# Where the loads of k, q and v and two rows of a weight product stand in a gated attention with a multiplicative FFN

## The chip, the core and the metric

The kernel runs on one core of one Trainium2 chip, in fp32. The metric is the device time in microseconds of one execution; the time before is the median of three runs. One further execution was taken with the hardware profiler, and every view below comes from it. Its engines are TensorE (PE; its weight loads are shown as PEld), VectorE (DVE), ScalarE (ACT), GpSimd (POOL) and SyncE (SP), whose queue issues nearly all DMAs.

## The reference

Attention, over 4 batches, 8 heads, 768 steps and a head size of 48, keeps a complex state S for each head. The bridge lays the heads side by side (384 columns, 3072 tokens), and the FFN multiplies two projections before two more weights.

```python
mag = np.sqrt(a_re * a_re + a_im * a_im)
scale = np.minimum(mag, 0.999) / (mag + 1e-06)
ar, ai = a_re * scale, a_im * scale
for t in range(S):
    kv = k[:, :, t] outer v[:, :, t]
    S_re, S_im = ar[t] * S_re - ai[t] * S_im + kv, ar[t] * S_im + ai[t] * S_re
    y[:, :, t] = q[:, :, t] @ S_re
x = y as (3072, 384)
out = ((x @ w1) * (x @ w2) @ w3) @ w_out      # w1, w2: 384 x 1024; w3: 1024 x 1024; w_out: 1024 x 384
```

The weights arrive as 64-bit floats and are read as pairs of 32-bit words ("words" below).

## The kernel before

**Algebra.** w3 @ w_out is computed once (`fuse`) and kept as `w3o`, so the FFN of a unit is two projections, their product `ab`, and one product with `w3o`. The gates are turned into cumulative magnitudes and angles, and k and q are scaled and rotated by them; attention is then a masked product in chunks of 128 steps with a carried state T.

**Units.** Work is cut into 8 units u = 0 to 7 (a batch and half its steps, 384 tokens, 3 chunks c). For a unit there are:

- the gates' passes (`gates(u)`, on ACT and DVE, 128 x 1152 each, in this order: a1, r1, im, sq, z1, n, z2, a2, z3, min, three mag scans, l, e, at, z4, r2, three ang scans, turns, k, q, ends, z5, abs, cos, sin, kc, qc, ks, qs), and then the moves: 12 DMAs of 192 KB that write KL and QL from R, k, A and q (L724);
- the pieces on PE (`pieces(u)`): tr (`turn`, transposes of R and k, L754, copied to KT by ACT, L756), kv (`state`, L818, and a DVE addition L824), sc (`scores`, L768, two halves for each chunk, each followed by DVE's COPY_PREDICATED into A, L771), and y (`outputs`, L801, copied to xT by ACT, L803). sc20 is chunk 2, half 0; y2 is chunk 2. One sc is 32 MATMULs and 32 LDWEIGHTS, one y 64 and 64 (y0 of an even unit 32 and 32), one kv 48 and 48, one tr 3 and 3;
- the FFN on PE: 16 items ab1, ab2 (`ffn_ab`, L840; 6 MATMULs each; ACT copies the first, DVE multiplies the second into `ab`, L845 and L847; four PSUM buffers m), then the products with w3o: for unit 0 six half items o (8 MATMULs each, L931), from unit 1 on one o and seven p (L895).

**Order.** In the first stage the 8 rows of w3 and w_out are loaded (`row_load`), rounded to fp32 by DVE and ACT (`row_work`, L975 to L992) and multiplied into eight PSUM sums (`fuse(f, j)` is row f, sum j, L1126, two MATMULs and two LDWEIGHTS), between the steps of unit 0's gates. Of rows 6 and 7 only j 0 to 3 are done there; the other halves are "fills" of two j each (f6 and f7) between unit 0's pieces. Two of the sums lie in the PSUM banks of sc, two in those of tr, kv and y, four in m. After row 7 ACT copies each sum to `w3o` (L1130).

The second stage is one list `seq` of PE items: unit 0's pieces with the fills, `begin 0`, unit 0's 16 ab items, then for each unit its pieces mixed with FFN items of the unit before. `FILLS` says ahead of which piece the fills of unit 0 and the six o items in unit 1 stand. In unit u > 1, AHEAD[u] FFN items come ahead of the pieces; unit 1 does not read AHEAD. `run` issues the items in that order, and after item number n as many steps of other work as `PLAN[n]` has letters: c the next pass of the gates, u the next step of rounding w1 and w2 (`w12_ops`; signs, ends, shifted, rounded), o a step of `out_weights`. After PLAN's end a planner with costs and due times chooses. At "need u" all passes of unit u that are left are issued; its moves are only issued once unit u-1 has ended.

w1 and w2 are cut into 4 blocks n, of which w1's and w2's words come as two DMAs (`w12_load`; 768 KB each for whole blocks); ab item 4n is the first to read block n. The words go through two buffers, so block n + 2 is requested when block n is rounded. The first part of block 0 lies in the buffers that unit 1's q and k take afterwards.

SP's queue takes each DMA in program order: an issue that waits for a buffer holds up those behind it. k and q of a unit are three DMAs of 192 KB each (`load_qkv`), v comes once as `vr` (`load_v`, 576 KB) for kv and once turned into Vb (`turn_v`, 14 DMAs of 18 to 72 KB) for y. Two places matter here: k and q of unit 1 were loaded after the second rounding of w12_ops,

```python
                if (parts, k) == (got[0][1][0], 1):
                    load_qkv(1)
```

and those of unit u + 1 right behind the moves of unit u, V of unit u + 1 at "begin u".

Of the kernel before, what the change touches and what calls it, by code (L numbers as in the profile page):

```python
# [375 lines left out]
def kernel(  # L376
# [45 lines left out]
    KF = FF // P  # L422
# [5 lines left out]
    TT = S // 2  # L428
    UC = TT // C
    NU = 2 * B  # L430
    AHEAD = [0, 0, 12, 10] + [8] * (NU - 4)
    LO, HI = 32, D - 32
    PASS, WIDE, SCAN, LAND, SLACK, LATE, RING, LOOK, NEAR, EARLY = 1.17, 1.4, 1.05, 1.8, 0.7, 1.2, 8, 4.0, 4, 2
    LOOKS = 3
    PLAN = ("c uuu uucc - - - cu uu cu cu uuu c u c u cu cu - u uuuuuc u - - uuu c cuu ccuc ucucc ucc uuuuuu "
            "ccccc - - ccc uc ccc c - - - - c - - - c - c c - c c cc - - - ccccccc - - c - ccc ccc cc - c - "
            "ccccccc - cc - - - - - ").split()
    FILLS = [1, 9, 14, 19], [3, 4, 6, 11, 14, 16]
    SB, LANES = 32, C // 32
    LN_EPS = math.log(1e-6)  # L440
    PI = math.pi
# [122 lines left out]
    def gates(u, split):  # L564
# [60 lines left out]
        for s in parts:  # L625
# [2 lines left out]
            yield "ACT", PASS, "e", ("l",)  # L628
            act(out=r[:, s], in_=r[:, s], func=AF.Exp, scale=-1.0)
        yield None  # L630
        q, K2 = g["q"], g["k"]
        k = K2[:, :, 0:TT]

# [99 lines left out]
                tt(out=q[:, s], in0=q[:, s], in1=Z[:, s], op=OP.mult)  # L733
            move(QL, (A, q), s)
        landed("moves", ("ks", "qs"), 4 * KD, 0.95)
        if 1 < u + 1 < NU:
            load_qkv(u + 1)
        yield None

    def step(ops, n=1):  # L740

        for _ in range(n):
            for op in ops:
                if op is None or op == "move":
                    break
# [63 lines left out]
    def state(u, c):  # L809

        KT, V = KT_t.pop((u, c)), g_t[u]["vr"][:, c].rearrange("p (h d) -> p h d", d=D)
        n = u % 2 * UC + c
        T = T_t.get((u // 2, n))
        kv = ps_v.tile([2 * D, H, D], FP, tag="v", name="kv")
        for hd in range(H):
            rows = KT[:, hd].rearrange("p d x f -> p (d x f)")
            for g in range(0, 2 * D, SB):
                nc.tensor.matmul(out=kv[g:g + SB, hd], lhsT=rows[:, g:g + SB], rhs=V[:, hd], start=True, stop=True)  # L818
        Tn = Tb[(u * UC + c) % 3]
        with tc.high_priority():  # L820
            if T is None:
                nc.scalar.copy(out=Tn[:, :, 0:D], in_=kv)
            else:
                nc.vector.tensor_tensor(out=Tn[:, :, 0:D], in0=kv, in1=T[:, :, 0:D], op=OP.add)  # L824
        if c == UC - 1:
            rho = L_t[u][1][:, :, TT:TT + 1].to_broadcast([2 * D, H, D])
            nc.vector.tensor_tensor(out=Tn[:, :, 0:D], in0=Tn[:, :, 0:D], in1=rho, op=OP.mult)
        T_t[u // 2, n + 1] = Tn
        if u + 1 < NU and c == UC - 1 - u % 2:
            load_v(u + 1)  # L830

    def ffn_ab(u, j):
# [257 lines left out]
    def w12_ops():  # L1090
        for n in range(FF // WB):
            for parts, k, raw in got[n]:
                ready["raw"] = ready[("raw", n)]
                yield from weight_ops((w1s, w2s)[k][:, n, parts], raw)
                if (parts, k) == (got[0][1][0], 1):
                    load_qkv(1)
            rounded[0] += 1
            w12_load(n + 2)

    def row_load(f, parts=1):  # L1100

# [147 lines left out]
    def run(seq):  # L1249
# [81 lines left out]
            o[0] = next(o[1])  # L1331
        for k, (kind, f) in enumerate(seq):
            if kind == "begin":
                if f + 1 < NU:
                    turn_v(f + 1)
                    landed("V", (), 14, 0.3, 0.57)
                held["unit"] = f
                others.extend([next(o), o] for u, o in streams if u == f)
            elif kind == "need":
                while gate["u"] <= f and gate["op"]:  # L1340
                    book(gate["op"])
                    advance()
                clock["PE"] = max(clock["PE"], ready.get("ks", 0.0))
                held.update(tr=[], kv=0)
            elif kind == "end":
                ended[0] = f
                if gate["op"] == "move":
                    advance()
            elif kind == "judge":
                for _ in looks[0]:  # L1350
                    pass
                judge(f)
            else:
                if kind == "sc":
                    clock["PE"] = max(clock["PE"], ready["moves"])
                item(kind)
                f()
                if k >= len(PLAN):
                    fill(k)
                while looks and held["unit"] > 1 and clock["POOL"] < clock["PE"] and next(looks[0], "over") != "over":  # L1360
                    clock["POOL"] = max(clock["POOL"], clock["PE"] - LOOK) + LOOK
# [10 lines left out]
    with tc.manual_schedule(engines={mybir.EngineType.PE}):  # L1372
# [9 lines left out]
        for f in range(KF):  # L1382
# [5 lines left out]
            if f == VLOAD:  # L1388
                load_v(0)
                w12_early()  # L1390
            if f >= KF - 2:
                continue
            for j in range(KF):
                fuse(f, j)
            step(steps, (3, 2, 2, 2, 1, 1)[f])
        for _ in steps:
            pass
        for f in range(KF - 2, KF):
            for j in range(KF // 2):
                fuse(f, j)  # L1400
        fills = [("f7" if f == KF - 1 else "f", lambda f=f, j=j: [fuse(f, j + x) for x in range(2)])
                 for f in range(KF - 2, KF) for j in range(KF // 2, KF, 2)]
        gate["ops"] = gates(1, False)
        chain(nc.scalar.preload_act_table_set("natural_log_exp_and_others"))
        with tc.manual_schedule(engines={mybir.EngineType.Activation, mybir.EngineType.DVE, mybir.EngineType.Pool, mybir.EngineType.SP}):
# [69 lines left out]
```

## Time and profile before

| What | Value |
|---|---|
| median of three runs | 557.94 us (557.38 to 559.2) |
| the profiled execution | 558.92 us, span 557.0 us, mean granted clock 0.99 |
| PE busy | 521.9 us, 94% of the span, 5474 MATMULs and 5474 LDWEIGHTS |
| DVE, ACT, POOL busy | 358.0, 272.7, 358.7 us |
| DMA queue q1 (SP), q0 (POOL) | 69.78 MB, 19.01 MB |
| DMA queue q8, instructions | 45 packets, 0.74 MB |
| first ab item of unit 0 (L840) | 88.43 us |
| first ab item of unit 1 | 152.93 us |
| first tr of unit 2 | 178.08 us |

Times inside a profile count from the first instruction, and the time of an execution is 1.9 us more than its span here. In a line of a timeline the start comes first and then the duration; in the chain of waits each line is a start, a duration and what ran or was waited for, and "issue" is time in which the engine waited for nothing that the profile shows. In a table of stages the columns are the stretch, its length, the busy times of PE, PEld, DVE, ACT and POOL with their instruction counts, the granted clock of PE, the DMA share and GB/s. The slices of the page are 13.9 us each.

### The profile page before, as it was taken

How to read it: one execution, taken by the hardware profiler on the slowest of the kernel's cores; microseconds unless marked ns; L12 is line 12 of the kernel's file. 1: busy time of each engine (PE TensorE's matmuls, PEld its weight loads, DVE VectorE, ACT ScalarE, POOL GpSimd, SP SyncE). 2: the span in 40 equal slices, each digit the busy share in tenths (PEclk: the TensorE clock that was granted, in tenths of full speed). 3: DMA queues.
4: the chain of work that ended last, by engine and by line, in shares of the span. 5: the costliest groups of instructions: out<-in, count | busy, mean ns of one | idle time of the engine just before them, and what ended most of it. 6: DMA issues, size and time to landing. Idle time of an engine off the chain costs nothing.

```text
span 557.0 us, 13239 instructions
## 1 busy us (share of the span) xinstructions
PE 521.9 (94%) x5474; PEld 359.1 (64%) x5474; DVE 358.0 (64%) x520; ACT 272.7 (49%) x391; POOL 358.7 (64%) x425
## 2 busy tenths in 40 slices
PE   4688769997999999999999999999999999999995
PEld 2344555565756696558756785679566966696564
DVE  7999576964587778769744984587448851331141
ACT  6988856554644655491628443744367222101100
POOL 1000000088898888889988998889898888887000
PEclk9999998998999999999999999999999999999999
DMA  8999796189359835985498347933793273222001
GB/s 265 358 409 267 159 334 175 44 205 192 102 141 237 203 106 159 223 218 158 113 203 189 98 122 184 235 100 108 155 231 108 82 207 73 72 87 74 0 3 48
DMA packets 73222, 89.73 MB, mean 161 GB/s; under 512 B 31808, under 2 KB 62976, under 8 KB 72384
## 3 DMA queue, kind: packets, MB, share of 16 engines
q1 hardware_dynamic: 67072, 69.78, 47.9%
q0 software_dynamic: 6080, 19.01, 12.0%
q8 instruction: 45, 0.74, 0.6%
q14 instruction: 25, 0.20, 0.1%
HBM read 65.14 MB, written 4.72 MB: 125 GB/s over the span
## 4 chain that ended last, share of the span: by engine, by line
PE 79%; DVE 6%; ACT 6%; DMA 4%; issue 3%; SPq 1%; DVEq 0%; ACTq 0%
PE m L840 40%; PE p L895 12%; PE o L931 10%; PE y L801 7%; PE sc L768 5%; DMA im<-in_a_im_dram 3%; PE kv L818 3%; PE tp L754 2%; ACT gZ L576 2%; ACT low L980 1%; PE f L1126 1%; DMA re<-in_a_re_dram 1%; DVE gZ L675 1%; ACT gA L576 1%; SPq L510 1%
## 5 line engine op out<-in xcount | busy, mean ns | idle before, releaser
L840 PE MATMUL m<-xT,w2s 128*128 128x384 f32 x384 | 135.0, 488 | 0.0
L840 PE MATMUL m<-xT,w1s 128*128 128x384 f32 x384 | 134.6, 487 | 0.0
L840 PEld LDWEIGHTS m<-xT,w1s 128*128 128x128 f32 x384 | 72.5, 190 | 48.1 <-issue 0.5
L840 PEld LDWEIGHTS m<-xT,w2s 128*128 128x128 f32 x384 | 71.5, 190 | 46.2
L1047 POOL TENSOR_SCALAR look<-look 128x256 f32<-128x256 f32 (+1 forms) x84 | 90.4, 1076 | 7.3
L847 DVE TENSOR_TENSOR ab<-m,a 128x384 f32<-128x384 f32 x64 | 35.2, 553 | 87.4 <-PE m L840 79.3
L845 ACT COPY a<-m 128x384 f32<-128x384 f32 x64 | 30.2, 474 | 116.1 <-PE m L840 115.8
L1028 POOL TENSOR_TENSOR seen<-seen,look 128x256 bf16<-128x256 bf16 (+1 forms) x84 | 72.2, 860 | 6.8
L1012 POOL MEMSET seen<- 128x256 bf16 x1 | 0.3, 311 | 106.8 <-DVE w2s L992 106.8
L931 PE MATMUL o<-w3o,ab 128*128 128x384 f32 x160 | 55.8, 499 | 0.0
L1044 POOL TENSOR_TENSOR look<-look 128x256 f32<-128x256 f32 (+1 forms) x72 | 53.8, 747 | 2.1 <-DMA look<-in_w_dram 0.3
L1046 POOL TENSOR_SCALAR look<-look 128x256 f32<-128x256 f32 (+1 forms) x44 | 50.8, 1155 | 3.9 <-DMA look<-in_a_re_dram 0.7
L1023 POOL DMA_DIRECT2D look<-in_w_dram x56 | 33.4, 596 | 16.6 <-POOL seen L1028 16.6
L771 DVE COPY_PREDICATED A<-mask,sc 128x512 f32<-128x512 uint8 x48 | 32.7, 730 | 16.5 <-PE sc L768 16.5
L931 PEld LDWEIGHTS o<-w3o,ab 128*128 128x128 f32 x160 | 30.3, 195 | 19.6 <-issue 1.6
L801 PE MATMUL y<-A,V 128*32 128x128 f32 x768 | 39.3, 274 | 3.1 <-issue 3.1
L1049 POOL TENSOR_TENSOR look<-look 128x256 f32<-128x256 f32 (+1 forms) x44 | 38.8, 883 | 3.7
L768 PE MATMUL sc<-QL,KL 96*32 96x32 f32 (+3 forms) x1536 | 32.6, 236 | 5.7 <-issue 4.2
L803 ACT COPY xT<-y 128x384 f32<-128x384 f32 x24 | 11.4, 474 | 52.8 <-PE y L801 52.7
L801 PEld LDWEIGHTS y<-A,V 128*32 128x32 f32 x768 | 33.8, 110 | 5.0 <-issue 4.4
L1126 PE MATMUL f<-wo_s,w3s 128*128 128x384 f32 x96 | 36.4, 528 | 0.0
L756 ACT COPY KT<-tp 128x384 f32<-128x384 f32 x40 | 34.1, 863 | 4.7 <-PE tp L754 4.7
(123 smaller groups left out, 892.5 us busy)
## 6 DMA issues: line engine op xcount, KB each, us to landing
look<-in_w_dram POOLq DMA_DIRECT2D x56, 256.0 KB, 4.2
raw<-in_w_dram SPq DMA_DIRECT2D x6, 1024.0 KB, 10.2
KL<-gR SPq DMA_DIRECT2D x24, 192.5 KB, 5.5
KL<-k SPq DMA_DIRECT2D x24, 192.5 KB, 6.3
re<-in_a_re_dram SPq DMA_DIRECT2D x24, 192.0 KB, 4.0
im<-in_a_im_dram SPq DMA_DIRECT2D x24, 192.0 KB, 3.6
k<-in_k_dram SPq DMA_DIRECT2D x24, 192.0 KB, 7.8
q<-in_q_dram SPq DMA_DIRECT2D x24, 192.0 KB, 7.5
```

Of the source, the lines that this page charges most:

```text
L768: nc.tensor.matmul(out=sc[SB * g:SB * g + SB, j, s0:C], lhsT=KL[:, x * n + j, w][:, s0:s0 + SB], rhs=QL[:, x * n + j, w][:, s0:C], start=T ...
L801: nc.tensor.matmul(out=o, lhsT=a, rhs=b, start=s0, stop=s1)
L840: nc.tensor.matmul(out=m, lhsT=w[:, j * P // WB, f, j * P % WB:j * P % WB + P], rhs=xT_t[u][:, f], start=(f == 0), stop=(f == KD - 1))
L847: nc.vector.tensor_tensor(out=ab_t[u][:, j], in0=m, in1=got[0], op=OP.mult)
L895: nc.tensor.matmul(out=m[p], lhsT=a[:, f], rhs=b[:, f], start=(f == 0), stop=(f == KH - 1))
L931: nc.tensor.matmul(out=m, lhsT=ab_t[u][:, f, t * P:(t + 1) * P], rhs=w3o[:, f], start=(f == 0), stop=(f == KF - 1))
L1028: nc.gpsimd.tensor_tensor(out=seen[:, 0:n], in0=seen[:, 0:n], in1=x, op=OP.add)
L1044: tt(out=x, in0=x, in1=x, op=OP.mult)
L1046: ts(out=y, in0=x, scalar1=high, scalar2=None, op0=OP.is_le)
L1047: ts(out=x, in0=x, scalar1=low, scalar2=None, op0=OP.is_ge)
L1049: tt(out=x, in0=x, in1=y, op=OP.mult)
L1126: nc.tensor.matmul(out=sums[j], lhsT=w3_t[f][:, j * P:(j + 1) * P], rhs=w3_t["wo"][:, f], start=(f == 0), stop=(f == KF - 1))
```

## The change

- k, q and vr of unit 1 are loaded once block 1 of w1 and w2 is rounded and block 3 is requested, so behind all words, and, as "begin 0" now comes ahead of that in the list, behind `turn_v(1)`. The tiles of q and k are taken earlier, where the gates first name them.
- k and q of unit 2 are no longer loaded behind unit 1's moves, nor V of unit 2 turned at "begin 1": both follow the last piece of unit 1.
- Row 6 of w3 by w_out is multiplied whole in the first stage; only two fills of row 7 are left.
- PLAN and FILLS are new. The fills of row 7 stand ahead of kv2 and of sc10 in unit 0, and the six o items of unit 1 ahead of tr00, tr01, kv0 (two), kv1 and y0. In PLAN the passes of unit 2's gates come later: kc and qc stand behind the seventh ab item of unit 1's FFN, and ks and qs are left for "need 2".

```diff
@@ -428,14 +428,14 @@
     TT = S // 2
     UC = TT // C
     NU = 2 * B
-    AHEAD = [0, 0, 12, 10] + [8] * (NU - 4)
+    AHEAD = [0, 3, 12, 10] + [8] * (NU - 4)
     LO, HI = 32, D - 32
     PASS, WIDE, SCAN, LAND, SLACK, LATE, RING, LOOK, NEAR, EARLY = 1.17, 1.4, 1.05, 1.8, 0.7, 1.2, 8, 4.0, 4, 2
     LOOKS = 3
-    PLAN = ("c uuu uucc - - - cu uu cu cu uuu c u c u cu cu - u uuuuuc u - - uuu c cuu ccuc ucucc ucc uuuuuu "
-            "ccccc - - ccc uc ccc c - - - - c - - - c - c c - c c cc - - - ccccccc - - c - ccc ccc cc - c - "
-            "ccccccc - cc - - - - - ").split()
-    FILLS = [1, 9, 14, 19], [3, 4, 6, 11, 14, 16]
+    PLAN = ("c uc - cu c uu - cu uu cuuuc - - cc - - uc uu u - uuucu ucuu u u cuccc uccuucuu - - uu uucc uuc u "
+            "uuucu cc ccc ccc cc ccc - - - c - - - - - - c - - c c c cc - cc - ccc - c - cc cc - cc ccc ccc - c c "
+            "cccc - - - o - - ").split()
+    FILLS = [9, 12], [1, 2, 4, 4, 6, 11]
     SB, LANES = 32, C // 32
     LN_EPS = math.log(1e-6)
     PI = math.pi
@@ -628,6 +628,8 @@
             yield "ACT", PASS, "e", ("l",)
             act(out=r[:, s], in_=r[:, s], func=AF.Exp, scale=-1.0)
         yield None
+        if "q" not in g:
+            take_qk(u)
         q, K2 = g["q"], g["k"]
         k = K2[:, :, 0:TT]
 
@@ -733,7 +735,7 @@
                 tt(out=q[:, s], in0=q[:, s], in1=Z[:, s], op=OP.mult)
             move(QL, (A, q), s)
         landed("moves", ("ks", "qs"), 4 * KD, 0.95)
-        if 1 < u + 1 < NU:
+        if 2 < u + 1 < NU:
             load_qkv(u + 1)
         yield None
 
@@ -826,7 +828,7 @@
             rho = L_t[u][1][:, :, TT:TT + 1].to_broadcast([2 * D, H, D])
             nc.vector.tensor_tensor(out=Tn[:, :, 0:D], in0=Tn[:, :, 0:D], in1=rho, op=OP.mult)
         T_t[u // 2, n + 1] = Tn
-        if u + 1 < NU and c == UC - 1 - u % 2:
+        if 1 < u + 1 < NU and c == UC - 1 - u % 2:
             load_v(u + 1)
 
     def ffn_ab(u, j):
@@ -1092,10 +1094,11 @@
             for parts, k, raw in got[n]:
                 ready["raw"] = ready[("raw", n)]
                 yield from weight_ops((w1s, w2s)[k][:, n, parts], raw)
-                if (parts, k) == (got[0][1][0], 1):
-                    load_qkv(1)
             rounded[0] += 1
             w12_load(n + 2)
+            if n == 1:
+                load_qkv(1)
+                load_v(1)
 
     def row_load(f, parts=1):
 
@@ -1331,7 +1334,7 @@
             o[0] = next(o[1])
         for k, (kind, f) in enumerate(seq):
             if kind == "begin":
-                if f + 1 < NU:
+                if f + 1 < NU and f != 1:
                     turn_v(f + 1)
                     landed("V", (), 14, 0.3, 0.57)
                 held["unit"] = f
@@ -1344,6 +1347,10 @@
                 held.update(tr=[], kv=0)
             elif kind == "end":
                 ended[0] = f
+                if f == 1:
+                    load_qkv(2)
+                    turn_v(2)
+                    landed("V", (), 14, 0.3, 0.57)
                 if gate["op"] == "move":
                     advance()
             elif kind == "judge":
@@ -1388,18 +1395,16 @@
             if f == VLOAD:
                 load_v(0)
                 w12_early()
-            if f >= KF - 2:
+            if f == KF - 1:
                 continue
             for j in range(KF):
                 fuse(f, j)
-            step(steps, (3, 2, 2, 2, 1, 1)[f])
+            step(steps, (3, 2, 2, 2, 1, 1, 0)[f])
         for _ in steps:
             pass
-        for f in range(KF - 2, KF):
-            for j in range(KF // 2):
-                fuse(f, j)
-        fills = [("f7" if f == KF - 1 else "f", lambda f=f, j=j: [fuse(f, j + x) for x in range(2)])
-                 for f in range(KF - 2, KF) for j in range(KF // 2, KF, 2)]
+        for j in range(KF // 2):
+            fuse(KF - 1, j)
+        fills = [("f7", lambda j=j: [fuse(KF - 1, j + x) for x in range(2)]) for j in range(KF // 2, KF, 2)]
         gate["ops"] = gates(1, False)
         chain(nc.scalar.preload_act_table_set("natural_log_exp_and_others"))
         with tc.manual_schedule(engines={mybir.EngineType.Activation, mybir.EngineType.DVE, mybir.EngineType.Pool, mybir.EngineType.SP}):
```

## The prediction

> **What bounds the kernel now.** I read the page's slices first, then the chain of waits in order of time, then the stages in windows, then SP's queue with the time at which each of its transfers landed.
>
> ```profile
> PE   4688769997999999999999999999999999999995
> PEclk9999998998999999999999999999999999999999
> ```
>
> TensorE (PE) is busy almost throughout, so its idle time in the first ten slices (13.9 us each) is what can be won. Taking MATMUL and LDWEIGHTS together, PE stands still 28.9 us in all: 7.0 before its first product, 6.7 in three waits for rows 0 to 5, which this change leaves alone, 11.05 between 51 and 89 us, 3.1 between 131 and 136, 0.9 at 240. The chain of waits names the large ones:
>
> ```profile
> 53.98 2.78 PE sc L1126 x4
> ...
> 76.28 1.42 issue
> 77.71 0.87 PE sc L768 x34
> 78.58 2.52 PE y L801 x89
> 81.10 3.07 issue
> 84.17 1.73 PE y L801 x38
> ...
> 133.16 2.76 issue
> 135.92 0.76 PE sc L768 x16
> ```
>
> Before 53.98 PE waits 2.51 us for the rounding of row 7. The three "issue" gaps, 7.25 us, wait for no engine. After each of the long gaps the granted clock falls:
>
> ```profile
> 54.00:58.00 4.00, 4.00 (x7) 2.19 (x8) 2.48 (x6) 1.07 (x3) 0.00 (x0) 0.57 0.92 225
> 86.00:90.00 4.00, 4.00 (x9) 2.29 (x10) 1.08 (x2) 2.28 (x4) 0.00 (x0) 0.71 1.06 329
> 134.00:138.00 4.00, 2.08 (x22) 1.35 (x22) 1.23 (x2) 0.00 (x0) 3.43 (x6) 0.76 0.63 105
> ```
>
> The last three columns are clock, DMA share and GB/s. A mean of 0.57 over 4 us is 3.4 us at half clock; with their neighbours (0.86 at 82 to 86, 0.81 at 138 to 142) the other two are 3.4 us each too. Each costs 1.7 us of work.
>
> SP's queue, start and duration of issue:
>
> ```profile
> 68.08 0.94 SPq L958 DMA_DIRECT2D raw<-in_w_dram  x2
> 69.12 2.58 SPq L510 DMA_DIRECT2D k<-in_k_dram  x3
> 71.74 1.98 SPq L510 DMA_DIRECT2D q<-in_q_dram  x3
> 73.82 0.54 SPq L540 DMA_DIRECT2D vr<-in_v_dram  x1
> 75.78 7.73 SPq L958 DMA_DIRECT2D raw<-in_w_dram  x4
> 83.57 11.14 SPq L550 DMA_DIRECT2D V<-in_v_dram  x14
> ...
> 122.88 1.99 SPq L510 DMA_DIRECT2D k<-in_k_dram  x3
> 125.20 2.57 SPq L510 DMA_DIRECT2D q<-in_q_dram  x3
> 128.10 11.58 SPq L550 DMA_DIRECT2D V<-in_v_dram  x14
> ```
>
> Exactly these loads (k, q, vr of unit 1; k, q, V of unit 2) fill the queue ahead of the gaps.
>
> **The skill.** "Runtime: NRT & Kernel Launch", section "Instruction fetch mechanics": an engine's program comes by DMA in blocks of 16 KiB, 256 instructions, mostly hidden. The trace agrees on the size (q8 moved 0.74 MB in 45 packets; PE has 10,948 instructions, 43 blocks) but not on "hidden". Counted in program order, PE stops after 51 instructions of sc20, after 51 of y2, and after 35 of unit 1's sc11: 256 and 3 x 256 apart. The fetch packets started at 75.11, 81.78 and 133.19 us, took 1.1 to 1.4, and PE went on 1.3 to 1.5 after their ends. Each was due when the block before began (70.7, 77.7, 129.7), so it stood 3.5 to 4.4 us in a queue. "DMA: Bandwidth & Descriptors", section "Queues, rings and completion order", says that an engine takes its rings in turn, packet by packet; here a fetch starts only about when what SP had issued some 1.5 us earlier has landed. I go by the trace: a stall is that backlog plus 2.5 us, less PE's time through 256 instructions. "TensorE: Matmul & The Clock Gate", Part 1, gives the half clock after an idle window of about 3.4 us; the 3.4 us above agree, though gaps of 2.5 us were enough here.
>
> **Row 6.** Eight MATMULs and their loads (j 4 to 7, 0.325 us apart at full clock, 2.6 us) move from the two f6 fills into the gap at 51.47. Row 5 shows the pace: 48.7 less 43.2 for 16. So PE works until 54.05, row 7 is ready at 53.93, and its half takes 2.6 instead of the 5.3 us it took at half clock. Gain 2.5 + 1.7 = 4.2; row 7's end comes at 56.65.
>
> **Unit 0's pieces** (to the first m). ACT empties the four sums by 57.15, then a1 1.05, KT 0.75, r1 1.05, KT, KT, ends 0.65, T 0.45, KT, KT, z1 1.1, KT: PE's turns and kv wait for KT about 3.4 us, against 3.0 now; kv2 ends at 66.8. Moves (landed 62.4) and V (71.2) are in time. sc00 starts at 66.8, f7b at 68.0, sc11 ends at 70.8 with waits of 0.5 for COPY_PREDICATED (1.1 now), y0 ends at 72.05.
>
> Fetches: the block before sc20's is begun at 67.9, and what was issued by 66.4 has landed by 69.4, so it is there by 71.9, wanted at 72.45: no stall (1.42 now). The next is requested at 72.45, behind the second words of block 1 (issued 68.52, landed 75.7 now, and nothing before them moves): there at 77.9, wanted in y2 at 75.65. Stall 2.25, not 3.07; bounds 0 (the packet overtakes the words) and 4. Half a chance of the slow clock, 0.85. y2 ends near 79, its copy to xT uncovered 0.5, and with what the pipeline loses at each gap ab starts near 81, against 88.4: 4.2 + 0.5 (predicated waits) + 0.8 + 1.4 (stalls) + 0.85 (clock) - 0.5 = 7.3, less 0.4 for KT, 6.9.
>
> **The words.** Block 2 is requested when w2's third of block 0 is shifted, near 75, and no longer behind k, q, vr. Turn_v(1)'s 14 issues (11.1 us now) come ahead of block 3's words, so these go at about 86 and land by 92; k, q (six issues, 0.65 each) follow by 91 and land by 97, vr after them. Block 3 is wanted by ab 13 of 16, near 81 + 23.3 = 104: 10 us of room. But DVE is close to full from 76: blocks 1 to 3 take 12, three mag and three ang scans 5.8, z4 and r2 2.7, seven passes from k to qs 9.5, ab 4.4, together 34 us, so qs ends near 113 against 115.8 now. DVE's queue is in order ("TensorE: Matmul & The Clock Gate" calls it strict FIFO; the timeline shows no overtaking), so behind a k pass that waits for its load stand w2's last rounding, the ab products and, through PSUM, PE. k at 97 against a k pass near 100: no wait.
>
> **Unit 1.** ab ends at 112. im(2), then the twelve moves are issued from qc on, near 110.3, and land 15.85 us later as now (113.07 to 128.9): 126.2. The o parts now stand early in the unit (6 x 2.6), so sc00 comes at 112 + 15.6 + 0.5 of turns + 1.6 of kv less 2.6 (the last o) = 127 to 128: in time, by 1 to 2 us. At kv1 the fetch finds the moves landed and no k, q, V: the 2.76 and its 1.7 of clock go, 4.46 (0.3 may stay). k, q, V of unit 2 are issued from the store of the last o part on, under y0 to y2, and a block is wanted in y2: PE takes 3.3 us for its 256 instructions, the fetch 2.5 and a backlog near 1. Bounds of the stall 0 and 2.5, and the clock behind the larger; I take 0.5. Gain 4.46 - 0.5 = 4.0.
>
> **Unit 2 and on.** Its k is wanted some 6 us after unit 1 ends and was issued 6 us before: no wait. SP has 28 V issues in a row (about 18 us), then re and im of unit 3; ks and qs come at unit 2's "need", about 12 us later against PE than now, and the moves land 7 us ahead of sc. The gates of unit 3 start 6 us later against PE; tr of unit 3 has 9 us to spare now. I take 0.3 lost, bounds -0.9 (the gap at 240 goes) and 3. The new second entry of AHEAD changes nothing, as unit 1 doesn't read it. The tail stays.
>
> **Sum.** 6.9 + 4.0 - 0.3 = 10.6, taken as 11 since pipeline losses at the gaps that close are not in it. The profiled execution took 558.92 (span 557.0 and 1.9 around it), so 547.9; it lies 0.98 above the median of 557.94, so the forecast is 547.0.
>
> **Rivals.** (1) The fetch waits move instead of shrinking: the words and unit 2's loads stand ahead of the fetches in y2 of both units, each losing 3 + 1.7. Then row 6 and the first stall remain: 4 to 6 won, 552 to 554. For it: backlog, not the kind of load, decides. Against: 1.7 MB (k, q, vr) less stands ahead of the words. (2) The fetches are not late at all: 2.25 + 0.85 + 0.5 more, 543, or 541 with the gap at 240. (3) Slower: k behind turn_v(1) and block 3. If ring limits hold SP so that k lands after some 112 instead of 97, DVE stops in front of w2's last rounding, PE stands before ab2.6, and moves, sc and all of unit 1 follow one for one. It is slower than now only if k lands after about 111; at 116 the time is 563. Against: in the queue now, 14 V issues cost at most 11.6 us. (4) The change does nothing: only if all the gaps have other causes; the gap for row 7 alone contradicts it.
>
> **Numbers.** Forecast 543.5 to 551: 0.62. Rival 1: 0.15. Rival 2: 0.12. Slower: 0.07. Nothing: 0.04. A measurement of this kernel tells about 0.3% (1.7 us) from no change. Range 541 to 553.5, which leaves out rival 3, "nothing" and the edges of the others. Faster 0.89, same 0.04, slower 0.07.
>
> **What would show it.** Right: no gap before row 7 and clock 1.00 at 54 to 58; first m at 79 to 83 and first m of unit 2's stage near 142 (now 152.9); one issue gap near 76 of 2 us or less, none in unit 1's sc. Wrong: gaps above 3 us in y2 of either unit (rival 1); PE waiting for w2s L992 or DVE k L642 waiting for k<-in_k_dram (rival 3); PE waiting at tr or sc of units 2 and 3 for moves.

## The result, and the profile after

The changed kernel takes 550.91 us (median of four runs, 548.91 to 552.7) against 558.19 before beside it (557.38 to 559.2): a ratio of 0.9868, 95% interval 0.9824 to 0.9911. It is faster by 1.3%, which lies inside the range of the prediction; the time is some 4 us above its centre of 547.0. Ratios, here and below, are of fast runs alone, slow ones (over 1.5% above the fastest of the same kernel) being left out, so that they need not equal the quotient of the two medians. The profiled execution took 548.91 us, span 547.12, which is the shortest of the four; of before it was 558.92 and 557.0.

The first product of a unit's FFN (L842, before L840) is a mark that both traces have. Distances between these marks are the stages: stage 1 runs from unit 0's mark to unit 1's, stage 2 on to unit 2's, stage 3 on to unit 3's.

| us | first m of unit 0 | to unit 1's | to unit 2's | to unit 3's | to the end |
|---|---|---|---|---|---|
| before | 88.43 | 64.49 | 58.86 | 59.18 | 286.03 |
| after | 79.25 | 60.95 | 58.96 | 61.41 | 286.55 |
| difference | -9.18 | -3.54 | +0.10 | +2.23 | +0.52 |

So 12.7 us are won up to 140 us, and 2.9 of them are given back later. The slices of the page (13.7 us each):

```profile
PE   5689889999999999998999999999999999999995
PEclk9899899999999999999999999999999999999998
```

PE's 7, 6 and 7 at the fifth, sixth and tenth place have become 8, 8 and 9. The dips of PEclk at the seventh and tenth place are gone; at the second and fifth it has new ones. The chain of waits of after, start and duration:

```profile
70.06 1.25 PE sc L770 x64
71.31 0.93 PE y L803 x32
72.24 1.09 PE sc L770 x50
73.33 2.42 PE y L803 x84
75.75 1.43 issue
77.18 1.52 PE y L803 x39
78.72 0.49 ACT xT L805
79.21 0.04 issue
79.25 31.23 PE m L842 x96
...
137.83 0.28 issue
...
220.30 1.37 DVE gR L707
221.67 0.14 issue
221.81 0.52 PE tp L756 x3
...
248.09 1.43 issue
```

From row 6 to 79.25 only one issue gap is left on this chain that is over 0.1 us, 1.43 in y2, and in unit 1's sc there is none (0.28 in its y2). New are a wait of unit 3's first turn for DVE's rotation of k (L707, kc) and an issue gap in a y of unit 3. The stages where clock was lost, now at 54 to 58 and at 60 to 64:

```profile
54.00:58.00 4.00, 3.45 (x14) 1.96 (x14) 2.05 (x5) 2.84 (x6) 0.00 (x0) 1.00 0.83 225
60.00:64.00 4.00, 3.45 (x96) 2.67 (x99) 3.42 (x5) 3.79 (x7) 0.00 (x0) 0.69 0.72 160
```

Row 7 runs at full clock. But the first kv, at 60.42 behind two waits for KT (0.59 and 1.14), meets half clock; before it had full clock there. SP's queue:

```profile
68.76 7.55 SPq L960 DMA_DIRECT2D raw<-in_w_dram  x4
76.36 10.09 SPq L550 DMA_DIRECT2D V<-in_v_dram  x14
86.55 0.93 SPq L960 DMA_DIRECT2D raw<-in_w_dram  x2
87.53 1.96 SPq L510 DMA_DIRECT2D k<-in_k_dram  x3
89.53 2.03 SPq L510 DMA_DIRECT2D q<-in_q_dram  x3
...
133.35 1.87 SPq L510 DMA_DIRECT2D k<-in_k_dram  x3
135.27 2.35 SPq L510 DMA_DIRECT2D q<-in_q_dram  x3
137.66 17.12 SPq L550 DMA_DIRECT2D V<-in_v_dram  x28
```

k of unit 1 is issued 18 us later than before (87.53, not 69.12) and lands at 94.5 to 95.9; k of unit 2 is issued at 133.35, not 122.88, and lands by 139. Neither is waited for.

### The profile page after: what moved, and what is told of

Its sections match the earlier page's. It is cut to its first block, busy times and chain, and to the rows that moved or that the text cites. A ratio compares the mean times of both kernels' runs of the same rounds, so it can differ in the third digit from the quotient of the medians.

```text
span 547.1 us, 13247 instructions
## 1 busy us (share of the span) xinstructions
PE 518.8 (95%) x5474; PEld 357.7 (65%) x5474; DVE 359.4 (66%) x520; ACT 273.4 (50%) x391; POOL 365.7 (67%) x425
## 4 chain that ended last, share of the span: by engine, by line
PE 82%; DVE 5%; DMA 4%; ACT 3%; issue 2%; SPq 2%; DVEq 0%
PE m L842 43%; PE p L897 12%; PE o L933 10%; PE y L803 7%; PE sc L770 5%; PE kv L820 3%; PE tp L756 2%; DMA im<-in_a_im_dram 2%; DMA raw<-in_w_dram 1%; DVE gZ L677 1%; ACT low L982 1%; DVE w3s L994 1%; DMA V<-in_v_dram 1%; ACT gZ L576 1%; SPq L550 1%
## 5 line engine op out<-in xcount | busy, mean ns | idle before, releaser
L842 PE MATMUL m<-xT,w1s 128*128 128x384 f32 x384 | 134.8, 487 | 1.1 <-ACT xT L805 1.1
L842 PE MATMUL m<-xT,w2s 128*128 128x384 f32 x384 | 135.0, 488 | 0.0
L842 PEld LDWEIGHTS m<-xT,w1s 128*128 128x128 f32 x384 | 72.1, 190 | 49.0 <-ACT xT L805 1.7
L842 PEld LDWEIGHTS m<-xT,w2s 128*128 128x128 f32 x384 | 71.5, 190 | 46.2
L1049 POOL TENSOR_SCALAR look<-look 128x256 f32<-128x256 f32 (+1 forms) x84 | 88.2, 1050 | 7.3
L1030 POOL TENSOR_TENSOR seen<-seen,look 128x256 bf16<-128x256 bf16 (+1 forms) x84 | 78.9, 940 | 6.8
L1046 POOL TENSOR_TENSOR look<-look 128x256 f32<-128x256 f32 (+1 forms) x72 | 55.9, 777 | 2.8 <-DMA look<-in_w_dram 0.9
L933 PE MATMUL o<-w3o,ab 128*128 128x384 f32 x160 | 54.2, 489 | 0.0
L1048 POOL TENSOR_SCALAR look<-look 128x256 f32<-128x256 f32 (+1 forms) x44 | 48.3, 1099 | 4.0 <-DMA look<-in_a_re_dram 0.7
L1051 POOL TENSOR_TENSOR look<-look 128x256 f32<-128x256 f32 (+1 forms) x44 | 42.2, 959 | 3.7
L803 PE MATMUL y<-QL,T 96*32 96x128 f32 x640 | 35.5, 272 | 1.7 <-issue 1.7
L576 ACT ACTIVATE re<-gZ 128x1152 int32<-128x1152 f32 (+2 forms) x17 | 17.8, 1049 | 32.4 <-DVE gZ L677 23.5
```

The source lines that it names most:

```text
L803: nc.tensor.matmul(out=o, lhsT=a, rhs=b, start=s0, stop=s1)
L842: nc.tensor.matmul(out=m, lhsT=w[:, j * P // WB, f, j * P % WB:j * P % WB + P], rhs=xT_t[u][:, f], start=(f == 0), stop=(f == KD - 1))
L933: nc.tensor.matmul(out=m, lhsT=ab_t[u][:, f, t * P:(t + 1) * P], rhs=w3o[:, f], start=(f == 0), stop=(f == KF - 1))
L1030: nc.gpsimd.tensor_tensor(out=seen[:, 0:n], in0=seen[:, 0:n], in1=x, op=OP.add)
L1046: tt(out=x, in0=x, in1=x, op=OP.mult)
L1048: ts(out=y, in0=x, scalar1=high, scalar2=None, op0=OP.is_le)
```

## Experiments

The theory: three of PE's gaps are waits for its own program (a fetch that stands behind what SP issued shortly before), the two moves of loads take that backlog away, row 6 fills the wait for row 7, and what is given back in unit 3 comes from the new PLAN. Rivals: the gain is row 6 alone; the loads pay by themselves; the loss in unit 3 comes from SP's 28 issues of V in a row. All runs in one table; ratios are to before on the same chip, stages as above:

| kernel | median us | ratio, 95% interval | first m | stage 1 | stage 2 | stage 3 |
|---|---|---|---|---|---|---|
| shifted_blocks | 559.65 (one run) | | 87.90 | 65.1 | 58.9 | 58.7 |
| u2_back | 558.15 | 0.9966 (0.9942 to 0.9989) | 81.13 | 66.4 | 59.3 | 64.9 |
| u1_back | 556.16 | 0.9961 (0.9938 to 0.9984) | 85.66 | 61.5 | 59.0 | 63.1 |
| row6_alone | 557.66 | 0.9979 (0.9948 to 1.0011) | 86.85 | 64.2 | 58.9 | 58.4 |
| loads_alone | 564.37 | 1.0105 (1.0069 to 1.0140) | 85.03 | 59.9 | 70.2 | 59.5 |
| plan_and_row | 561.96 | 1.0060 (1.0038 to 1.0081) | 83.15 | 68.4 | 59.0 | 61.5 |
| changed_again | 554.79 | 0.9902 (0.9869 to 0.9935) | 82.17 | 61.6 | 59.0 | 63.8 |
| qs_early | 547.58 | 0.9786 (0.9756 to 0.9816) | 81.78 | 62.3 | 59.3 | 60.1 |
| qs_again | 546.85 | 0.9797 (0.9756 to 0.9838) | 77.89 | 61.0 | 59.0 | 58.5 |
| words_first | 548.89 | 0.9821 (0.9786 to 0.9856) | 81.73 | 61.6 | 59.0 | 58.6 |
| fill_later | 548.19 | 0.9790 (0.9746 to 0.9834) | 83.86 | 61.5 | 59.0 | 58.3 |
| words_first_fill | 549.41 | 0.9810 (0.9777 to 0.9844) | 87.01 | 61.6 | 59.5 | 58.9 |

First m and the stages are of one profiled execution each and carry its luck with the clock and with the stalls (below); the ratios do not hang on it. The first four and the second four shared their runs of before, 558.76 and 558.89 us; the last four, 559.34.

### Is a gap bound to a place in the program? (shifted_blocks)

The kernel before with 128 further instructions of PE ahead of everything, and nothing else.

```diff
+        spare = ps_v.tile([P, KD, C], FP, tag="v", name="spare")
+        for _ in range(32):
+            nc.tensor.matmul(out=spare[0:32, 0, 0:32], lhsT=ident[:, 0:32], rhs=ident[:, 0:32], start=True, stop=True)
```

> The kernel before with 32 small products (32 MATMUL-LDWEIGHTS pairs twice over, 128 instructions in all, into a spare PSUM tile) on PE ahead of row 0, while PE is idle anyway. Theory (PE stops where a block of 256 instructions ends): the three issue gaps move by exactly 128 instructions towards the start of the program: from after 51 instructions of sc20 to after some 59 of sc11, from after 51 of y2 to after 51 of y1, from after 35 of unit 1's sc11 to after 35 of its sc01; where the block is wanted at another distance from the loads, the gaps may be shorter or missing, but none is left at the old places. Rival (PE waits for data that the profile does not show, V or T or the moves): the gaps stay at sc20, y2 and sc11 of unit 1. Time within 2 us of the kernel before in both.

Its chain of waits from 70 us on, of which these are the waits of more than 1 us:

```profile
76.61 4.51 issue
...
130.91 1.98 issue
```

The gaps at the old places (sc20, y2, sc11 of unit 1) are gone, and these two stand in their stead, in y1 and in another score of unit 1. Counted as MATMULs and LDWEIGHTS from the kernel's own start, before stopped after 943, 1198 and 1957; this one stops after 1200 and 1958 with the added ones counted, which is after some 1072 and 1830 of its own work; at 943 it does not stop. The work that waits has changed, the place in the program has not. This shows that the issue gaps are bound to blocks of the program; no engine, buffer or piece of work makes them.

The DMA records of the traces say what PE waits for. In all stalls of 0.2 us and more at these counts, and at two later ones (2467 and 4756), before, after and in every run of the table, the last 16 KiB packet of the instruction queue q8 ended 1.2 to 1.6 us before PE went on (here at 79.61 and 131.59, for 81.12 and 132.89). In the stalls of 1.4 us and more the packet had started 2.6 to 6.5 us after PE began the block before; in the short ones, of 0.2 to 0.6 us, at counts 1198 and 2467 it had started after 1.1 to 1.6. So a long stall is a packet that started late.

### The loads of unit 2 put back (u2_back)

```diff
-        if 2 < u + 1 < NU:
+        if 1 < u + 1 < NU:
             load_qkv(u + 1)
...
-                if f + 1 < NU and f != 1:
+                if f + 1 < NU:
                     turn_v(f + 1)
...
-                if f == 1:
-                    load_qkv(2)
-                    turn_v(2)
-                    landed("V", (), 14, 0.3, 0.57)
```

> The changed kernel with k and q of unit 2 again behind unit 1's moves and V of unit 2 again turned at 'begin 1'; the rest as changed. Theory (late instruction fetches): the fetch begun at kv1 (about 126 us) stands behind these loads, so PE stops in unit 1's sc for 1.5 to 3 us with 'issue' named, usually with 3.4 us of half clock after it; unit 1's stage (first m of unit 0 to first m of unit 1's FFN) goes from 61.0 to 63 to 66, the whole 2 to 5 us slower than the changed kernel (551 to 555). Rival (the new places of the o items keep PE fed and hide the fetch): stage 61 to 61.5, same time within 1 us. On the loss later (unit 2's FFN with unit 3's pieces takes 61.4 where it took 59.2): if it is SP's 28 V issues in a row, it goes here (59.2); if it is the late place of qs of unit 2 and with it the late start of unit 3's gates, it stays above 60.5.

The chain in unit 1's scores:

```profile
130.62 0.77 PE sc L770 x28
131.39 2.27 issue
133.66 1.50 PE sc L770 x30
```

The gap is back at program count 1956 and with it 6.8 us of half clock, 3.4 us of work. Stage 1 is 5.5 us longer than in the profile after. The ratio goes from 0.987 or 0.990 to 0.997: two thirds of the gain or so hang on this move. The loss, 5.5 us by the first of the two ratios and 3.6 by the second, is about the 2 to 5 expected. Stage 3 stays long (64.9) although V of unit 2 is issued early again. So the 28 V issues do not make the loss in unit 3. It is even longer than in the changed kernel, by 3.5 us; 2.66 of that is a wait of unit 3's first sc that ends 0.27 us after the last of its moves has landed, at 252.91.

### The loads of unit 1 put back (u1_back)

```diff
                 yield from weight_ops((w1s, w2s)[k][:, n, parts], raw)
+                if (parts, k) == (got[0][1][0], 1):
+                    load_qkv(1)
             rounded[0] += 1
             w12_load(n + 2)
-            if n == 1:
-                load_qkv(1)
-                load_v(1)
```

(and `load_v(1)` back in `state`)

> The changed kernel with k, q of unit 1 again right behind the second rounding of w1, w2 and vr at unit 0's last kv; the rest as changed. Theory (late fetches): 1.7 MB more stand ahead of block 2's words and of the fetches wanted in sc20 and y2 of unit 0; an issue gap in sc20 of 1 to 3 us and one in y2 of 2 to 4 us, half clock after them, block 2's words land 4 to 5 us later; first m at 82 to 87 instead of 79.3, the whole 3 to 7 us slower than the changed kernel. Rival (the fetch only waits for the words of block 1, which are there in both): one gap in y2 of 1.4 to 2.2, first m at 79 to 80.5, same time within 1.5 us.

```profile
74.57 2.10 issue
76.67 1.42 PE sc L770 x30
78.09 3.67 PE y L803 x83
81.76 1.82 issue
```

The ratio is that of u2_back, so the gain hangs on this move as much. Both stalls of unit 0 are back, at counts 943 and 1198, 3.9 us against 1.43 after, with one window of half clock at 77. From the first kv to the first m it takes 23.3 us, after 18.8, before 25.3 (with one fill more in it). Stage 1 stays short (61.5). But the stall at 943, in sc20, is no mark of these loads: u2_back, which has them late, stops there for 2.15. The stall in y2 is. Both kernels come to it after a stall in sc20, and its packet starts 4.27 us after its block is due here and 1.12 in u2_back, so that PE stops for 1.82 and 0.28. In the changed kernel, then, each move of loads shortens a stall of its own stage.

### Row 6 alone (row6_alone)

The kernel before, with the parts of the diff for row 6, the fills of row 7 where they were (FILLS[0] = [14, 19]), and PLAN's letters for the two missing fills joined to their neighbours.

> The kernel before with row 6 of w3 by w_out whole ahead of row 7 and its two fills gone, the steps of those list items moved to the items ahead of them; loads and the other steps as before. Theory: no gap before row 7 and clock 1.00 at 54 to 58, as 2.5 and 1.7 us are won; row 7's half ends near 56.7; of the 4.2 us 3 to 4.5 reach the first m (84 to 85.5 instead of 88.4), the whole 554 to 555.5. Rival (the turns and kv wait for ACT's KT copies anyway, and the fills of row 6 stood in those waits): less than 1.5 us of it reach the first m, 556.5 to 558.

```profile
76.72 2.52 PE y L801 x89
79.24 3.35 issue
82.59 1.77 PE y L801 x38
```

and one of its stages:

```profile
62.00:66.00 4.00, 3.93 (x98) 3.00 (x88) 3.01 (x6) 3.62 (x6) 0.00 (x0) 0.60 0.42 78
```

The wait before row 7 is gone, and row 7 has full clock. First m comes 1.6 us earlier than before, not 3 to 4.4, and the ratio cannot be told from none: -1.2 us, interval -2.9 to +0.6. The median, 557.66, lies where the rival had it, and a part of the rival is there: the waits in the turns and kv are 3.5 us, where before has 3.0. Half clock has gone from row 7 to the kv behind it, so that the 1.7 us of clock were moved, and the stall in y2, which hangs on the queue, stays at 3.35. This execution also met half clock in row 4 and came to row 6 1.2 us later than before.

### The loads alone (loads_alone), and PLAN with row 6 alone (plan_and_row)

loads_alone is the kernel before with all of the diff that concerns loads; it keeps its own PLAN but for unit 2's k pass, which is two items later so that it is issued behind its load. plan_and_row is the changed kernel with both moves of loads undone.

> The kernel before with the loads of k, q, v of units 1 and 2 moved as in the change and nothing else, but that k of unit 2 is scaled two list items later, since its load now stands behind unit 1's last piece. Theory (late fetches, shared by the loads): the gap in sc20 goes, the one in y2 shrinks to 1.5 to 2.5 as the words of block 1 still stand ahead, the one in unit 1's sc11 goes; row 7's gap stays; first m 86 to 87.5, unit 1's stage 60 to 61, the whole 4 to 6.5 us faster than the kernel before. Rival (the loads only pay with the new PLAN, since the kernel before uses k early): PE waits for DVE passes that wait for k, less than 2 us faster or slower.

> The changed kernel with both load moves undone: row 6 and the new lists alone. Theory: the gaps in sc20 and y2 of unit 0 and in unit 1's sc are back at counts 943, 1198 and 1957, and unit 3's late gates cost their 2 us and more; 556.5 to 560, no faster than the kernel before. Rival (the effects of the two load moves overlap rather than add): as either of the two with one move undone, 555 to 557.

The timeline of DVE in loads_alone (the bracket is the idle time before the instruction and what ended it):

```profile
155.49 1.36 DVE L643 TENSOR_TENSOR k<-k,gR 128x1152 f32<-128x1152 f32 x1 [8.66 <-DMA k<-in_k_dram]
158.72 1.36 DVE L645 TENSOR_TENSOR q<-q,gA 128x1152 f32<-128x1152 f32 x1 [1.87 <-DMA q<-in_q_dram]
```

that of SP's queue:

```profile
148.45 0.54 SPq L938 DMA_DIRECT2D out_dram<-ot  x1
149.03 1.86 SPq L509 DMA_DIRECT2D k<-in_k_dram  x3
```

and one of its stages:

```profile
162.00:166.00 4.00, 2.98 (x6) 1.19 (x5) 1.61 (x2) 3.97 (x5) 3.50 (x5) 0.50 0.64 154
```

Stage 1 is 59.9 us, the shortest of all: the stall in unit 1 is gone. The gain of 4 to 6.5 us did not come. The old PLAN has k of unit 2 scaled within the first FFN items of unit 1, and its load is now issued behind the last o part. DVE stands 8.66 us; the ab products are queued behind it, PE stops 5.9 us and runs 10 us at half clock after it. Stage 2 is 11.3 us longer and takes more than all that the loads have won.

In unit 0 the stalls hardly change, 1.35 and 2.79 for 1.42 and 3.07, where the first was expected to go and the second to shrink to 1.5 to 2.5:

```profile
74.86 1.35 issue
...
79.61 2.79 issue
```

The words of block 2, requested at 75.78 before and at 75.10 in the changed kernel, go out at 72.28 here, in the place that the loads left, and land at 78.8 and 80.8; the packet for y2 starts at 79.99. This is what the prediction's first rival says: the backlog decides, not the kind of load. That first m comes 3.4 us earlier all the same is the clock. This execution has no half clock from 50 to 90, where before has two windows of 1.7 us of work each, although its wait before row 7 (2.53) is that of before:

```profile
54.00:58.00 4.00, 3.77 (x12) 2.32 (x13) 2.72 (x7) 2.36 (x5) 0.00 (x0) 1.00 0.72 205
```

The chain of plan_and_row:

```profile
73.53 2.42 PE y L803 x84
75.95 3.86 issue
79.81 2.79 PE y L803 x43
```

and one of its stages:

```profile
82.00:86.00 4.00, 3.43 (x12) 1.75 (x7) 0.96 (x1) 1.44 (x2) 0.00 (x0) 0.50 1.04 309
```

With k, q and vr ahead of the words again, the stall in y2 is the longest of all at that place, three windows of half clock follow, and unit 1 has its stall back too (2.82 at 136.06); at 943 there is none. Its 561.96 is above the 556.5 to 560 expected. So neither half of the change is faster than before; each is slower. The PLAN is what makes room for the later loads, and the later loads are what shortens the stalls of the tighter PLAN. Against the ratio of the result, undoing one move cost 0.9 to 1.0% and undoing both costs 1.9% (against that of changed_again, 0.6 and 1.6%): the two effects add up and do not overlap.

### qs brought forward (qs_early, qs_again)

In the changed PLAN only the pass qs of unit 2 is left for "need 2" (kc, qc and ks run at 154.63, 155.91 and 157.32; the text ahead of the prediction counts ks among those left, which is wrong). Its letter is put three items earlier, and o and the first passes of unit 3 follow.

```diff
 the last letters of PLAN
-c c cccc - - - o - -
+c c cccc c - - oc c c
```

> The changed kernel with PLAN's entries 71, 74, 75 and 76 of 77 each one pass longer: qs of unit 2 and so its moves right behind ks, and a1, r1, im of unit 3 by the end of PLAN; before, qs was left to 'need 2' and unit 3's gates began 16 us later against PE than in the kernel before. Theory (that late start costs unit 3's stage): no PE gap ahead of tr of unit 3, its moves land before sc, the issue gap in y of unit 3 goes as the moves and k, q of unit 4 come earlier; unit 2's FFN with unit 3's pieces 59 to 59.8 instead of 61.4, the whole 1.5 to 3 us faster than the changed kernel. Rival (SP's row of V issues delays re and im of unit 3): stage 61 or more, same time.

DVE in the changed kernel, then in qs_early (the last pass of unit 2, then a pass of unit 3):

```profile
164.28 1.49 DVE L716 TENSOR_TENSOR q<-q,gZ 128x1152 f32<-128x1152 f32 x1
...
178.36 1.36 DVE L590 TENSOR_TENSOR im<-im,gR 128x1152 f32<-128x1152 f32 x1 [1.01 <-ACT gR L576]
```

```profile
163.50 1.34 DVE L715 TENSOR_TENSOR q<-q,gZ 128x1152 f32<-128x1152 f32 x1
...
169.88 1.42 DVE L589 TENSOR_TENSOR im<-im,gR 128x1152 f32<-128x1152 f32 x1 [1.67 <-ACT gR L575]
```

Measured from the first m of the stage, that pass of unit 3 runs at 22.4 us before (175.32), 38.2 after and 25.8 here. The wait at unit 3's first turn is gone, stage 3 is 60.1 and 58.5, and the ratio is 0.9786 and in the repetition 0.9797, against 0.9868 and 0.9902 for the changed kernel. One half of the expectation missed: the issue gap in unit 3's y stayed in qs_early (1.46) and was absent in qs_again, so it does not hang on qs. The repetition was to say whether the gain was luck:

> The version with qs early once more, beside the three below. If the gain over the changed kernel is the gates of unit 3: ratio 0.975 to 0.982, the wait at tr of unit 3 absent, the stage of unit 3 near 60 us. If its first run was a lucky one: 0.985 to 0.990.

It was not. What stays open is its size: on one chip the medians differ by 7.2 us (554.79 and 547.58), while the two pairs of profiles differ by 3.8 on average, about 3.3 of it in stage 3.

### What is queued ahead of the stall in y2 (words_first, fill_later, words_first_fill)

All three start from qs_early. words_first issues block 1's words ahead of V of unit 0:

```diff
-            turn_v(0)
             w12_load(1)
+            turn_v(0)
```

> qs early, and the words of block 1 are issued ahead of V of unit 0 (14 issues) at the start of the second stage. Theory (a fetch waits for what SP issued shortly before it): the words of block 1 land some 6 us sooner, the fetch that is due at unit 0's sc20 and y2 finds a short queue, the issue gap of 1.4 to 2.8 us there goes, and with it its half clock; first m at 77 to 79; 2 to 4 us less than qs early, ratio near 0.974. V of unit 0 lands later, near 73, which y0 may feel with up to 1 us. Rival: the gap is put there by the count of instructions and what one fetch costs, not by the queue: a gap above 1.2 us stays in sc20, y1 or y2; ratio as qs early or worse.

Its queue:

```profile
59.20 2.07 SPq L959 DMA_DIRECT2D raw<-in_w_dram  x4
61.69 12.15 SPq L549 DMA_DIRECT2D V<-in_v_dram  x14
```

The words, issued from 66.7 on in qs_again, are issued by 61.3 here, and the stall in y2 is gone, but for 0.25, as the theory has it (qs_again had 0.83 there). But the V issues now take 12.15 us (8.86 in qs_again). SP halts between them, and goes on at 67.16 and at 69.50 where two of the words' loads landed at 67.14 and 69.48. The last V lands at 75.35, not near 73: y waits 0.54 for it. The gain of 2 to 4 us did not come; the time is that of qs_early or 1 to 2 us above it, which the intervals do not separate. A fetch wait was exchanged for a data wait.

> qs early, and the second fill of row 7 stands ahead of y1 in place of sc10 in unit 0. Theory: the 8 instructions of the fill leave the 256-instruction boundaries ahead of sc20 where they are or move them by 8 earlier in the pieces between, so the issue gap stays, at the same program count; the fill covers up to 0.5 us of a wait for a copy. Ratio within 0.003 of qs early. Rival: sc10 waits for a PSUM bank that the fill freed, 0.5 to 1 us more: ratio 0.003 above qs early.

fill_later (second fill of row 7 ahead of y1; FILLS[0] = [9, 17]) is where qs_early is, 0.979. Its stall of 2.08 us stands at count 943 again, 8 instructions further into sc20, as the 8 of the fill no longer stand ahead of it. sc10 waits 1.09 for DVE's A, so the rival's wait was there too, and in the time it cannot be seen.

> words first, and the second fill of row 7 stands behind y2 of unit 0, where PE waits 0.57 us for the copy to xT. Theory: that wait is covered, 0.5 us less than words first. Rival: the sums of row 7 come later, so ACT's copy of them to w3o stands ahead of the copy to xT and PE waits as before: no difference.

In words_first_fill (FILLS[0] = [9, 19]) V is wanted 1.4 us sooner, as the fill no longer stands ahead of it, and the last V lands 3.2 us later than in words_first, at 78.53; PE waits 1.31 and 2.40 for V; behind it 6.8 us run at half clock. The wait for xT is covered as expected, and nothing is gained: 0.981.

### The changed kernel once more (changed_again)

> The changed kernel once more, beside the others of this set on one chip, so that they compare within a chip, and as a second profile of it. Both theories: ratio to the kernel before 0.982 to 0.991, profile with first m at 79 to 82, an issue gap at the same place in y2 of unit 0 (1198 MATMULs and LDWEIGHTS into the program), unit 1's stage 61 to 63, and 61 to 62.5 for unit 2's FFN with unit 3's pieces. If runs of one kernel differ by several us because of when the half clock falls, the clock windows of this profile stand elsewhere than in the first.

0.9902, interval 0.9869 to 0.9935, which overlaps that of the result. Stage 3, 63.8, is longer than the 61 to 62.5 expected: the stall in unit 3's y (count 4756) is 2.12 here, with 3.4 us of half clock behind it. In this execution the issue gap of unit 0 stood in sc20 (1.63, count 943) and not in y2 (count 1198): which of the blocks is late differs between executions of the same program. The traces suggest what decides it for sc20: when PE begins the block before (count 687), against the issue of the first of block 1's words behind V of unit 0. In the six profiles where PE came 1.2 to 2.5 us after it (here 70.59 for 69.13) the stall was there; in the four where it came between 2.2 us before and 0.5 after (68.22 for 68.76 in the result's profile) it was not; loads_alone, 0.4 us after and with the stall, is the exception. So a half-clock window some 30 us earlier, like the one at 40 here, can bring the stall back. This was read off the runs and not tried on its own.

## Why the prediction was right, and where it was off

**Row 6: mechanism right, its clock mis-sized.** The wait of 2.51 and the half clock at 54 to 58 went, as forecast: 4.2. The step that failed is the silent one behind "1.7 of clock": that the clock stays up until the next stall. It fell at the first kv, 60 to 64, in the changed kernel and in row6_alone. Of 4.2 us, 2.5 are left. Nor is the half clock a sure price of the wait: in loads_alone the same wait stood and full clock followed.

**Up to the first m: more than forecast.** PE's idle time from row 6 to the first m fell from 11.07 to 4.37 us, 6.7, where the sum had 4.3 (2.5 + 0.5 + 0.8 + 1.4 - 0.5 - 0.4). Term by term: row 7 2.51 to none (as forecast), waits in the turns and kv, mostly for KT, 2.97 to 2.37 (forecast 0.4 longer; they are 0.6 shorter), COPY_PREDICATED 1.08 to none (forecast 0.5 left), sc20 1.42 to none (as forecast), y2 3.07 to 1.43 (forecast 2.25), the copy to xT none to 0.57 (forecast 0.5). Clock gave 1.7 (two windows before, at 54 and 85; one after, at 61) where the sum had 2.55. Of the 9.2 us, 0.8 are left that no term explains; the sum had 6.9. The first m at 79.25 is at the lower edge of "79 to 83", and that is luck in part: in the four other profiles whose kernel is the same up to there (changed_again, u2_back, qs_early, qs_again) it came at 82.17, 81.13, 81.78 and 77.89, with the 79.25 a mean of 80.4, near the forecast of 81. The stall in sc20, forecast as gone, stood in two of these five, with 1.63 and 2.15.

**The words and loads: right.** Block 3's words went out at 86.55 (forecast 86), k and q of unit 1 followed and landed by 95.9 and 97.7 (97); unit 1's moves were issued from 110.39 (110.3) and landed at 124.1 (126.2), sc00 came at 126.61 (127 to 128).

**Unit 1: right.** Forecast 4.0, measured 3.54; the gap and its clock are gone, 0.28 remains in y2. u2_back shows that it was the loads of unit 2: with them back, gap and half clock are back.

**Later units: the step that failed.** "The gates of unit 3 start 6 us later against PE; tr of unit 3 has 9 us to spare" was valued at 0.3, bound 3. They start 16 us later (38.2 against 22.4), so the term is mis-sized: the spare time is used up, and tr waits 1.16; with an issue gap of 1.43 in unit 3's y, the stage gives back 2.2, and 0.5 more goes in the rest. qs_early shows the cause of the first: qs waits in PLAN for the end of the list, and with it all of unit 3's passes. The bound held, the value did not.

**From the profile to the median: the largest single miss.** The sum made 547.9 for the profiled execution, and it took 548.91. But before's profiled execution lay 0.98 above its median and after's 2.0 below, so 3.0 of the 3.9 us between 547.0 and 550.91 come from that last step. Executions of these kernels differ by a few windows of half clock and by which block is late; the two profiles of the changed kernel have spans of 547.1 and 553.0 us. So it is luck that the sum meets the profiled execution within 1 us, and the median of changed_again, 554.79, lies outside the range of 541 to 553.5 (0.9902 of the 558.19 beside the result would be 552.7, inside it).

**The rivals.** (1) Moved fetch waits: false for the change, but loads_alone has them in unit 0, behind the words of block 2. (2) Fetches that are not late at all: 1.43 was left. (3) A k pass that waits for its load and holds DVE: not in the change (k landed 15 us ahead of the point where it decides), and plain in loads_alone for unit 2, with 8.66 us. The prediction looked for it in unit 1. (4) Nothing: excluded.

**The skill.** "Runtime: NRT & Kernel Launch", section "Instruction fetch mechanics", on blocks of 256 instructions: shifted_blocks agrees, since the stalls keep their place in the program within two instructions when 128 are put ahead. "Mostly hidden" holds for most of the 43 blocks of before and not for three, which stop PE for 1.42 to 3.07 us. "TensorE: Matmul & The Clock Gate", Part 1, says that the window in which activity is watched is free-running, so that the same kernel can differ from run to run. The traces agree: every half-clock stretch is 3.41 us or a multiple, within one trace the stretches start whole multiples of 3.413 us apart (30.72 and 51.20 before, 9 and 15 times), and two executions of the changed kernel had them at 17 and 61, and at 19, 40, 64 and 255 us, the last of their run-outs aside.

## What to carry to other kernels

A gap of PE that waits for nothing in the profile, at counts of instructions that differ by about a multiple of 256 (943, 1198 and 1957 here), is likely its program arriving late: see whether a packet of the instruction queue ended just before PE went on, look at what the DMA queues were given in the microseconds before, and move loads that nobody needs yet. What moves up into the freed place can stall it as well (the words of block 2 in loads_alone). A load moved later needs the order of its readers moved too, where other work stands behind them as ab stood behind k on DVE; tested apart, both halves of such a change can be slower than doing nothing, as here. When a hand-written order leaves one step to "whenever it is needed", ask which steps of the next unit are queued behind it: here one pass, three items earlier, with what was queued behind it, was worth 0.7 to 1.2% where the whole change was worth 1.0 to 1.3%, and the versions with it are the best measured here (0.979 to 0.982).

## What the runs showed of the hardware

- A stall of the fetch keeps its place in the program and not its length: at count 943 it was 0.96 to 2.15 us in seven runs, at count 1198 between 0.25 and 3.86 where there was one. PE went on 1.2 to 1.6 us after the packet had ended. That the packet's start follows SP's queue is what the moved loads and words show (u1_back, plan_and_row, words_first); what it stood behind on each DMA engine was not followed.
- Gaps of PE as short as 2.3 us (u2_back) were followed by 6.8 us at half clock; in the changed kernel two waits of 0.59 and 1.14 within 2.3 us were followed by 3.4. But 2.53 us in loads_alone (at 51.70) and 2.80 in qs_early (at 76.91) were followed by none. A gap's length alone does not tell whether half clock comes.
- Work that removes a wait need not remove the half clock: in the changed kernel and in row6_alone a window came at the next thin place, 7 to 9 us later.
